# Attention with a hard score cut, then an eight-expert layer: where the value products of a pair of heads stand in the loop

## The chip, the cores and the metric

The kernel runs on one NeuronCore of a Trainium2 chip. The metric is the device time of one execution in microseconds (us). The engines of the core run side by side, each through its own list of instructions in order: TensorE (PE in the profile; PEld are its weight loads), VectorE (DVE), ScalarE (ACT), GpSimd (POOL) and SyncE (SP, which here only issues transfers).

## The reference

Two layers in a row. First attention over 8 batches x 8 heads, 576 positions, 64 wide, in which every score that lies more than `tau` under the largest of its row is dropped; then a layer of 8 experts, each of which takes at most 576 of the 4608 rows.

```python
# attention, per batch and head: q, k, v are [576, 64]
scores = scale * np.matmul(q, k.T)
thresh = np.max(scores, axis=-1, keepdims=True) - tau
scores = np.where(scores >= thresh, scores, -1e9)
attn = np.exp(scores - max); attn = attn / (sum + 1e-9)
x = attn @ v                      # the heads side by side: [4608, 512]
# experts
logits = x @ w_gate               # [4608, 8]; the best (row, expert) pairs first, 576 rows per expert
for e in range(8): out[mask_e] = np.maximum(x[mask_e] @ w1[e], 0) @ w2[e]
```

## The kernel before, in words

**Pairs, tiles and slots.** Two heads make a pair, so there are 32 pairs `p`, four to a batch `b`. The scores of a pair are worked in 9 tiles of 128 rows x 576 columns: eight full ones (128 queries of one head) and a short one, tile 8, with the last 64 queries of both heads. In all 288 tiles. The loop at the end of `attention` handles two tiles in one turn, a slot, numbered `s_`; two pairs are 18 tiles or 9 slots, so everything repeats every 9 slots, and below B is `9*(p//2)`: the even pair's short tile is scored in slot B+2, the odd one's in B+6, and the next two pairs begin at B+9.

**A tile's way.** TensorE writes the scores into PSUM (`sc`, line 69). VectorE multiplies them into SBUF with the row's extreme beside them (`z`, `nb`, line 74), ScalarE takes the exponential (line 86), VectorE zeroes what lies under the cut and sums the row (`pp` or `pm`, line 90), TensorE transposes the result in 64x64 blocks (`tb`, line 98), ScalarE copies that to `pt` (lines 113 and 115). One stage of a tile falls in one slot, the next in the slot after it or the one behind that. On TensorE a slot reads: scores of two tiles, in four slots of nine some left-over transposes (`left`, into spare columns of `sc`), value products, sometimes a small job, then the transposes of two older tiles.

**Value products.** The output of a pair, transposed, is made in two column halves `f`, of 256 and 320 queries, each with a PSUM bank of its own (`xo0`, `xo1`; `xo` in the profile). A half takes four *units* (`pv_unit`, line 146: two matmuls, one for each head, with 128 rows of keys and 64 output columns of the array) and its share of the *group* (`pl_unit`, line 154: four matmuls of 64x64 that add the last 64 keys, two for each half; their operand `pl` is copied out by ScalarE at lines 125, 127 and 128, the last of it in slots B+5 and B+9). When the group is through, ScalarE copies both banks to `xt` (line 155).

**What sets their order.** `push_pair` writes the units and the group of a pair into a queue when the pair's fourth tile has come back from the transposes, each with a condition (`when`) on the tiles that it needs. `columns` takes entries from the queue's head once a slot, behind the scores. The number that it takes is worked out from what is left of the pair and the slots up to `last_slot`, and it stops behind the group, which closes the pair. A unit that opens a half waits, in the program, until the bank's last reader stands in the list (`free_v`). Once a batch is through, small jobs (`aux`: the logits `lg_unit` twice, lines 173 and 175; two transposes `lgt_unit`, `lgm_unit`, lines 185 and 195; in the first two batches five `xt_unit`, line 207) run through `xo1` as well, one a slot, in slots where `xo1` is free (`whole`). What they leave in PSUM is read in the next slot, by ScalarE or VectorE (lines 178 to 217), ahead of that slot's line 74. The reads of the banks are put on their engines by `flush`, behind the scores of the next slot.

The last of the value products, the last logits and the sorting of rows to experts follow on each other; then comes the expert layer, which the change does not touch.

Of the kernel before, what the change touches and what calls it, by code (L numbers as in the profile page):

```python
# [13 lines left out]
AF = mybir.ActivationFunctionType  # L14
# [8 lines left out]
def attention(ctx, tc, qk, vl, tau, wgd, xrows, xts, Lg, nb_batches, ident, swap, R, after_first):  # L23
    nc=tc.nc
    V=nc.vector; A=nc.scalar; G=nc.gpsimd; T=nc.tensor
    NP=nb_batches*4; NT=NP*9
# [10 lines left out]
    LD={}  # L37
# [57 lines left out]
    PT={}; PL={}; TB={}  # L95
# [36 lines left out]
    have={}  # L132
# [3 lines left out]
    def bank_v(sh,n):  # L136
        banks[n].append([False])
        return ps_v.tile(sh,F32,name="xo%d"%n)
    def free_v(n): return banks[n][-1][0]
    def pv_unit(p,f,u):  # L140
        b,j=divmod(p,4)
        if b not in XT: XT[b]=wk.tile([128,4,S],F32,name="xt",bufs=XTB)
        if u==0: XO[p,f]=bank_v([128,512],f)
        xo=XO[p,f]; q=FQ[f]; v=LD[p]["v"]
        for h in range(2):
            T.matmul(xo[64*h:64*h+64,:q.stop-q.start],v[:,f,128*u+64*h:128*u+64*h+64],PT[p][:,h,u,q],start=(u==0),stop=False,skip_group_check=True)  # L146
    def pl_unit(p,fs=(0,1)):

        b,j=divmod(p,4); r=[]
        for f in fs:  # L150
            xo=XO.pop((p,f)); q=FQ[f]; n=q.stop-q.start
            for a in range(2):
                g=slice(64*a,64*a+64); h=a^f
                T.matmul(xo[64*h:64*h+64,:n],LD[p]["v"][g,f,512:576],PL[p][g,q],start=False,stop=True,skip_group_check=True)  # L154
            r.append((banks[f][-1],lambda xo=xo,q=q,n=n: A.activation(XT[b][:,j,q],xo[:,:n],AF.Copy)))
# [47 lines left out]
    def xt_unit(b,c,k=1):  # L203
        ps=bank_v([128,4,128],k)
        n=128 if c<4 else 64
        for j in range(4):
            T.transpose(ps[:n,j],XT[b][:,j,c*128:c*128+n],ident)  # L207
        early=b<nb_batches-NDEF-NBO
        if early: xr=wk.tile([128,XW],F32,name="xr",bufs=XRB)
        else: xr=wk.tile([128,2,S],F32,name="pp",bufs=PPB)[:,0,:XW]  # L210
        def ev():
            src=RD[b][:,:,2*c:2*c+2] if c<4 else RD["m",b][0:64]
            fv=xr[:n,512:XW].rearrange("p (j h) -> p j h",j=4); xv=xr[:n,:512].rearrange("p (j d) -> p j d",j=4)
            if early:
                V.tensor_copy(xv,ps[:n]); G.tensor_scalar(fv,src,1.0,0.0,op0=ALU.mult,op1=ALU.add)  # L215
# [10 lines left out]
    def push_pair(p):  # L226
        b,j=divmod(p,4)
        def when(n): return lambda: have.get((p,n),1<<30)+HOLD<=st["slot"]
        if p==NP-1:


            def left(f):
                for k,g in pl_unit(p,(f,)): g(); k[0]=True
            for f in range(2):
                for u in range(4): queue.append(("c",when("t3" if f==0 else "t8"),0 if u else f+1,lambda f=f,u=u: pv_unit(p,f,u),p))
                if f==0: queue.append(("n",when("t8"),False,lambda: rd_calc(b),p))
            for g in (lambda: left(0),lambda: left(1),lambda: lg_unit(b,0)(),lambda: lg_unit(b,1)(),lambda: lgt_unit(b)(),lambda: lgm_unit(b)()):
                queue.append(("n",when("pl"),False,g,p))
            queue.append(("n",lambda: not later,False,lambda: late.extend([lambda k,c=c: xt_unit(b,c,k) for c in range(5)]),p))
            return  # L240
        for f in range(2):
            for u in range(4): queue.append(("c",when("t3" if f==0 else "t8"),0 if u else f+1,lambda f=f,u=u: pv_unit(p,f,u),p))
# [12 lines left out]
    def flush():  # L255
        for k,g in later: g(); k[0]=True
        later.clear()
    def last_slot(p): return 9*(p//2)+(12 if p%2 else 8 if p<NP-2 else 7)
    def columns(all=False):
        c=[x[4] for x in queue if x[0]=="c"]  # L260
        if not c: n=9
        else: n=9 if all else max(1,c.count(c[0])//max(1,last_slot(c[0])-st["slot"]+1))
        while queue and queue[0][1]():
            k,_,first,g,p=queue[0]
            if k=="c":
                if n==0: return
                if first and not free_v(first-1): return
                n-=1
            queue.pop(0); r=g()
            if k=="c" and r:  # L270
                later.extend(r)
                return
    def whole():
        if aux and free_v(1) and st["slot"]>=st["last"]+aux[0][0]:
            r=aux.pop(0)[1](); st["last"]=st["slot"]
            later.append((banks[1][-1],r))

# [679 lines left out]
```

## Time and profile before

| | |
|---|---|
| time, median of 3 runs | 1000.09 us (997.43 to 1001.54) |
| the profiled execution | 1003.83 us, span 1001.9 us |
| attention's slots with TensorE full | 42.77 to 452.68 us |
| busy over the span | PE 964.3, DVE 781.2, ACT 633.0, POOL 261.9 us |
| mean granted TensorE clock | 0.983 |

Busy shares are over the whole program, of which attention's loop is a little under half; the stage itself is read by windows. A matmul of this kernel shows as two records, because each fp32 matmul makes two passes; so `x8` behind a group of rows is four matmuls. Matmuls overlap in the records: what one costs is read from the start of one row to the start of the next, not from its length. `64*128`, `64*64` and `128*64` ahead of a matmul's shape are the rows x columns of the array that it occupies.

### The profile page before, as it was taken

Reading aid. Unit: us, or ns where it says so; the run is one execution under the profiler, and the core shown is the slowest. Engines: PE = TensorE matmul, PEld = TensorE weight load, DVE = VectorE, ACT = ScalarE, POOL = GpSimd, SP = SyncE. Lnnn points to the kernel's source line nnn. Section 1 sums busy time; section 2 is a strip of 40 time slices with the busy share of each in tenths; the row PEclk is TensorE's granted clock in tenths of the full one; section 3 lists DMA queues with packets and bytes.
Section 4 is the critical chain, followed back from the end, with each engine's and each line's share of the span. In section 5 each row is a group of like instructions: output and inputs, shape, how many; then the busy total and the mean of one; then the engine's idle time right before and its main releaser. Section 6 shows DMA issues by size and latency. Waiting matters only on the chain.

```text
span 1001.9 us, 24115 instructions
## 1 busy us (share of the span) xinstructions
PE 964.3 (96%) x9141; PEld 710.4 (71%) x9141; DVE 781.2 (78%) x2158; ACT 633.0 (63%) x1257; POOL 261.9 (26%) x411
## 2 busy tenths in 40 slices
PE   7999999999999999998789999999999899999996
PEld 4555655655565555565679798897988879898895
DVE  7999999999999999995669778687787587525220
ACT  6899888888899898986545354253442344545340
POOL 2333443444233333330020213221303003220202
PEclk9999999999999999999979999999999899999998
DMA  6332251451533333203750605242434325241101
GB/s 250 97 119 84 83 182 58 177 184 61 176 111 120 99 117 106 97 3 141 260 199 20 224 30 183 84 152 93 153 106 135 120 70 172 100 156 56 40 11 42
DMA packets 35858, 116.98 MB, mean 117 GB/s; under 512 B 4384, under 2 KB 5024, under 8 KB 35232
## 3 DMA queue, kind: packets, MB, share of 16 engines
q1 hardware_dynamic: 28352, 92.85, 27.1%
q0 software_dynamic: 5888, 19.03, 6.0%
q10 hardware_dynamic: 1504, 3.59, 1.2%
q8 instruction: 72, 1.18, 0.5%
q14 instruction: 42, 0.34, 0.1%
HBM read 93.01 MB, written 21.38 MB: 114 GB/s over the span
## 4 chain that ended last, share of the span: by engine, by line
PE 84%; DVE 8%; issue 3%; DMA 2%; ACT 1%; another core or an unknown queue 0%; POOLq 0%; SPq 0%; DVEq 0%; ACTq 0%
PE pf L787 21%; PE pf L819 19%; PE sc L69 13%; PE xo L146 13%; PE tb L98 8%; DVE pp L90 2%; PE xo L154 2%; PE pt L732 2%; DVE z L74 2%; PE xo L207 1%; PE rps L440 1%; PE xo L173 1%; DMA out_dram<-y,idx 1%; PE sc L98 1%; DVE cmp L372 1%
## 5 line engine op out<-in xcount | busy, mean ns | idle before, releaser
L75 POOL TENSOR_SCALAR nb<-nb,taub 128x1 f32<-128x1 f32 x288 | 152.6, 530 | 286.2 <-DVE z L74 235.5
L86 ACT ACTIVATE pp<-z,nb 128x576 f32<-128x576 f32 x256 | 193.3, 774 | 39.6 <-DVE z L74 39.1
L74 DVE TENSOR_SCALAR_CACHE_REDUCE z<-sc 128x576 f32<-128x576 f32 x288 | 205.7, 750 | 14.6 <-PE sc L69 13.8
L90 DVE SCALAR_TENSOR_TENSOR pp<-z,nb,pp 128x576 f32<-128x576 f32 x256 | 199.8, 812 | 0.3
L819 PE MATMUL pf<-w2h,H 128*128 128x512 f32 x576 | 195.2, 402 | 0.7 <-DVE H L372 0.7
L69 PE MATMUL sc<-qk 64*128 64x288 f32 (+1 forms) x1280 | 181.2, 427 | 3.4 <-DVE z L74 1.5
L146 PE MATMUL xo<-pt,vt 128*64 128x320 f32 (+1 forms) x1024 | 155.7, 420 | 0.4 <-DVE xr L215 0.3
L113 ACT ACTIVATE pt<-tb 128x512 f32<-128x512 f32 x256 | 139.2, 589 | 3.3 <-PE tb L98 1.7
L819 PE MATMUL pf<-w2l,H 128*128 128x512 f32 x320 | 128.3, 401 | 0.0
L826 POOL DMA_INDIRECT out_dram<-y,idx x40 | 42.8, 1069 | 317.7 <-ACT y L822 244.2
L819 PEld LDWEIGHTS pf<-w2h,H 128*128 128x128 f32 x576 | 106.5, 189 | 21.5 <-DVE H L372 1.6
L69 PEld LDWEIGHTS sc<-qk 64*128 64x128 f32 (+1 forms) x1280 | 93.8, 179 | 33.7 <-DVE z L74 5.7
L98 PEld LDWEIGHTS tb<-ident,pp 64*128 64x128 f32 x2048 | 75.4, 139 | 58.0 <-ACT pp L86 20.1
L787 PE MATMUL pf<-xh,w1h 128*128 128x288 f32 (+2 forms) x512 | 112.0, 306 | 0.7 <-ACT xh L733 0.7
L787 PE MATMUL pf<-xl,w1h 128*128 128x288 f32 (+2 forms) x512 | 111.7, 304 | 0.0
L787 PE MATMUL pf<-xh,w1l 128*128 128x288 f32 (+2 forms) x512 | 111.7, 304 | 0.0
L822 ACT ACTIVATE y<-pf 128x512 f32<-128x512 f32 x40 | 23.9, 597 | 128.8 <-PE pf L819 125.3
L146 PEld LDWEIGHTS xo<-pt,vt 128*64 128x64 f32 x1024 | 60.7, 136 | 57.7 <-issue 27.4
L98 PE MATMUL tb<-ident,pp 64*128 64x64 f32 x2048 | 94.1, 229 | 5.0 <-ACT pt L113 4.8
L799 ACT ACTIVATE hf<-pf 128x576 f32<-128x576 f32 x56 | 36.5, 651 | 96.0 <-PE pf L787 83.0
L787 PEld LDWEIGHTS pf<-xh,w1h 128*128 128x128 f32 x512 | 83.9, 194 | 1.5 <-ACT xh L733 1.1
L787 PEld LDWEIGHTS pf<-xh,w1l 128*128 128x128 f32 x512 | 83.6, 193 | 0.2
(199 smaller groups left out, 1315.5 us busy)
## 6 DMA issues: line engine op xcount, KB each, us to landing
qk<-qk_dram SPq DMA_DIRECT2D x31, 864.0 KB, 4.7
vt<-vl_dram SPq DMA_DIRECT2D x32, 576.0 KB, 5.1
w2s<-w_dram SPq DMA_DIRECT2D x32, 512.0 KB, 5.5
w1s<-w_dram SPq DMA_DIRECT2D x28, 512.0 KB, 5.7
xrows<-pp SPq DMA_DIRECT2D x24, 260.0 KB, 2.8
xts<-xt SPq DMA_DIRECT2D x2, 1152.0 KB
pt<-xts SPq DMA_DIRECT2D x2, 1152.0 KB, 8.1
xrows<-xr SPq DMA_DIRECT2D x8, 260.0 KB, 2.0
```

Source lines behind the costliest of these rows:

```text
L69: T.matmul(sc[o,f,:HS], kd["q",h][r,c], kd["k",h][r,:],start=True,stop=True)
L74: V.tensor_scalar(z,SC.pop(t)[:,:,:HS],-0.125,None,op0=ALU.mult,op1=ALU.min,accum_out=nb[:,0:1])
L75: G.tensor_scalar(nb[:,1:2],nb[:,0:1],taub[:,0:1],None,op0=ALU.add)
L86: A.activation(pview(t),ZB[t].rearrange("p a b -> p (a b)"),AF.Exp,bias=NBI[t][:,0:1],scale=-1.0)
L90: V.scalar_tensor_tensor(pv,ZB.pop(t).rearrange("p a b -> p (a b)"),NBI[t][:,1:2],pv,op0=ALU.is_le,op1=ALU.mult,accum_out=den_of(p)[:,p%4, ...
L98: g=slice(64*r,64*r+64); T.transpose(o[:,r],x[r%len(x)][g],ident[g,g])
L113: A.activation(PT[p][:,i%2,:,(i//2)*128:(i//2+1)*128].rearrange("p k (r q) -> p r k q",r=2),tb,AF.Copy)
L146: T.matmul(xo[64*h:64*h+64,:q.stop-q.start],v[:,f,128*u+64*h:128*u+64*h+64],PT[p][:,h,u,q],start=(u==0),stop=False,skip_group_check=True)
L787: T.matmul(ps[:,h,:n],s[w][:,k,f*128:(f+1)*128],s[x][:,k,cols[h]],start=(i==0),stop=(i==11))
L799: A.activation(hf,ps[:,:,:HS],AF.Relu)
L819: T.matmul(ps[:,0,:],H[:,f,c:c+128],s[w][:,f],start=(f==0 and j==0),stop=e)
L826: G.indirect_dma_start(out=out,out_offset=IOA(ap=s["idx"][:n,t:t+1],axis=0),in_=y[:n],in_offset=None)
```

## The change

Each entry of the queue now carries the slot from which it may run, in place of its pair, and `columns` takes what is due. In each of the 9 slots there are two units, or one unit and the group: the even pair has its first half in slots B+4 and B+5, the group and one unit in B+6, two units in B+7 and one in B+8; the odd pair begins in B+8 with one unit, has two in B+9, one of each half in B+10, the group and one unit in B+11 and two units in B+12. The group stands in the slots that score a short tile (B+6 of its own two pairs, and B+11, which is slot B+2 of the next two), and it is the first thing behind the scores. It now closes the first half and opens the second one. The short tile is scored second in both cases; before, the even pair's was scored first. A half is copied out by itself, the first in the slot behind the group, the second in the slot behind its last unit. The last pair keeps its way: all units as soon as they can run, the group at the end. The number of matmuls, copies and transfers stays.

```diff
+    def evict(p,f):
+        b,j=divmod(p,4); xo=XO.pop((p,f)); q=FQ[f]
+        return banks[f][-1],lambda: A.activation(XT[b][:,j,q],xo[:,:q.stop-q.start],AF.Copy)
+    def open_v(p,f):
+        new=(p,f) not in XO
+        if new: XO[p,f]=bank_v([128,512],f)
+        return XO[p,f],new
-    def pv_unit(p,f,u):
+    def pv_unit(p,f,u,last):
...
-            T.matmul(xo[...],v[...],PT[p][:,h,u,q],start=(u==0),stop=False,skip_group_check=True)
-    def pl_unit(p,fs=(0,1)):
+            T.matmul(xo[...],v[...],PT[p][:,h,u,q],start=new,stop=last,skip_group_check=True)
+        if last:
+            if f==1: have[p,"pv"]=1
+            return [evict(p,f)]
+    def pl_unit(p,fs,last=()):
...
-                T.matmul(xo[...],LD[p]["v"][g,f,512:576],PL[p][g,q],start=False,stop=True,skip_group_check=True)
-            r.append((banks[f][-1],lambda xo=xo,q=q,n=n: A.activation(XT[b][:,j,q],xo[:,:n],AF.Copy)))
-        have[p,"pv"]=1
-        return r
+                T.matmul(xo[...],LD[p]["v"][g,f,512:576],PL[p][g,q],start=new,stop=f in last,skip_group_check=True)
+        return [evict(p,f) for f in last]
...
+        def v(f,u,at,last=False,first=False): queue.append(("c",when("t8" if f else "t3"),f+1 if first else 0,lambda: pv_unit(p,f,u,last),at))
+        B=9*(p//2)
...
-        for f in range(2):
-            for u in range(4): queue.append(("c",when("t3" if f==0 else "t8"),0 if u else f+1,lambda f=f,u=u: pv_unit(p,f,u),p))
-            if (f,j)==(0,3): queue.append(("n",when("t8"),False,lambda: rd_calc(b),p))
-        queue.append(("c",when("pl"),False,lambda: pl_unit(p),p))
+        for u in range(4): v(0,u,B+((8,9,9,10) if p%2 else (4,4,5,5))[u],False,u==0)
+        if j==3: queue.append(("n",when("t8"),0,lambda: rd_calc(b),p))
+        if p%2: v(1,0,B+10,False,True)
+        queue.append(("c",when("pl"),0 if p%2 else 2,lambda: pl_unit(p,(0,1),(0,)),B+(11 if p%2 else 6)))
+        for u in range(p%2,4): v(1,u,B+((0,11,12,12) if p%2 else (6,7,7,8))[u],u==3)
...
-    def last_slot(p): return 9*(p//2)+(12 if p%2 else 8 if p<NP-2 else 7)
     def columns(all=False):
-        c=[x[4] for x in queue if x[0]=="c"]
-        if not c: n=9
-        else: n=9 if all else max(1,c.count(c[0])//max(1,last_slot(c[0])-st["slot"]+1))
+        n=0
         while queue and queue[0][1]():
...
-                if n==0: return
-                if first and not free_v(first-1): return
-                n-=1
+                if not all and st["slot"]<at: return n
+                if first and not free_v(first-1): return n
+                n+=1
-            if k=="c" and r:
-                later.extend(r)
-                return
+            if k=="c" and r: later.extend(r)
...
         p8=[(t//9,n) for n,x in enumerate((tr_,ev_)) for t in x if t%9==8]
+        if sc_ and sc_[0]%9==8: sc_.reverse()
         for t in sc_: score(t)
```

In the lists below a unit's matmuls stand at line 146 before and 152 now, the group's at 154 and 162, the copies of the banks at 155 and 142, the small transposes' reads at 190, 191, 200, 201 and 196, 197, 206, 207. Here `x2` counts matmuls of two heads, so `x2` of `xo<-pt,vt` is one unit.

TensorE, slots B+6 to B+8 of pairs 2 and 3, from the scores of the odd pair's short tile, before:

```order
L69 MATMUL sc<-qk 64x288 x4
L146 MATMUL xo_831<-pt,vt 64x256 x2
L146 MATMUL xo_930<-pt,vt 64x320 x2
L98 MATMUL tb<-ident,pp 128x64 x16
L69 MATMUL sc<-qk 128x288 x4
L146 MATMUL xo_930<-pt,vt 64x320 x4
L98 MATMUL tb<-ident,pp 128x64 x16
L69 MATMUL sc<-qk 128x288 x4
L98 MATMUL sc<-ident,pp 128x64 x6
L146 MATMUL xo_930<-pt,vt 64x320 x2
L154 MATMUL xo_831<-pl,vt 64x256 x2
L154 MATMUL xo_930<-pl,vt 64x320 x2
```

and now:

```order
L69 MATMUL sc<-qk 64x288 x4
L162 MATMUL xo_831<-pl,vt 64x256 x2
L162 MATMUL xo_932<-pl,vt 64x320 x2
L152 MATMUL xo_932<-pt,vt 64x320 x2
L98 MATMUL tb<-ident,pp 128x64 x16
L69 MATMUL sc<-qk 128x288 x4
L152 MATMUL xo_932<-pt,vt 64x320 x4
L98 MATMUL tb<-ident,pp 128x64 x16
L69 MATMUL sc<-qk 128x288 x4
L98 MATMUL sc<-ident,pp 128x64 x6
L152 MATMUL xo_932<-pt,vt 64x320 x2
L152 MATMUL xo_1028<-pt,vt 64x256 x2
```

The group has moved up by two slots to the short tile's scores, and the next pair's first unit has moved into slot B+8.

TensorE, slots B+10 to B+12 of the same two pairs (B+11 scores the next even pair's short tile), before:

```order
L146 MATMUL xo_1074<-pt,vt 64x256 x4
L98 MATMUL tb<-ident,pp 128x64 x16
L69 MATMUL sc<-qk 64x288 x4
L69 MATMUL sc<-qk 128x288 x2
L146 MATMUL xo_1170<-pt,vt 64x320 x4
L98 MATMUL tb<-ident,pp 128x64 x16
L69 MATMUL sc<-qk 128x288 x4
L146 MATMUL xo_1170<-pt,vt 64x320 x4
L154 MATMUL xo_1074<-pl,vt 64x256 x2
L154 MATMUL xo_1170<-pl,vt 64x320 x2
```

and now:

```order
L152 MATMUL xo_1028<-pt,vt 64x256 x2
L152 MATMUL xo_1126<-pt,vt 64x320 x2
L98 MATMUL tb<-ident,pp 128x64 x16
L69 MATMUL sc<-qk 128x288 x2
L69 MATMUL sc<-qk 64x288 x4
L162 MATMUL xo_1028<-pl,vt 64x256 x2
L162 MATMUL xo_1126<-pl,vt 64x320 x2
L152 MATMUL xo_1126<-pt,vt 64x320 x2
L98 MATMUL tb<-ident,pp 128x64 x16
L69 MATMUL sc<-qk 128x288 x4
L152 MATMUL xo_1126<-pt,vt 64x320 x4
```

The short tile now stands behind the full one, and the group stands between it and the units in place of at the end of B+12.

The end of attention, VectorE, from the reads of the seventh batch's first small transpose (`lw`) to those of its second (`lwm`), before:

```order
L190 TENSOR_TENSOR lw<-xo_7058,rd 128x4x32 x2
L191 TENSOR_REDUCE Lg<-lw 128x32
L74 TENSOR_SCALAR z,nb<-sc 128x576 x2
L90 SCALAR_TENSOR_TENSOR pp,den<-z,nb,pp 128x576 x2
L200 TENSOR_TENSOR lwm<-xo_7111,rm 64x64
L201 TENSOR_REDUCE Lg<-lwm 64x8
```

and now:

```order
L197 TENSOR_REDUCE Lg<-lw 128x32
L74 TENSOR_SCALAR z,nb<-sc 128x576 x2
L90 SCALAR_TENSOR_TENSOR pp,den<-z,nb,pp 128x576 x2
L74 TENSOR_SCALAR z,nb<-sc 128x576 x2
L90 SCALAR_TENSOR_TENSOR pp,den<-z,nb,pp 128x576 x2
L74 TENSOR_SCALAR z,nb<-sc 128x576 x2
L90 SCALAR_TENSOR_TENSOR pm_100,den<-z,nb,pm_100 128x576
L90 SCALAR_TENSOR_TENSOR pp,den<-z,nb,pp 128x576
L74 TENSOR_SCALAR z,nb<-sc 128x576 x2
L90 SCALAR_TENSOR_TENSOR pp,den<-z,nb,pp 128x576 x2
L206 TENSOR_TENSOR lwm<-xo_7254,rm 64x64
L207 TENSOR_REDUCE Lg<-lwm 64x8
```

The second read comes four slots behind the first in place of one, since `xo1` is now in use in slots B+10 to B+12; it falls in a slot B+5. On ScalarE the copies of the second-last pair's two banks stood together ahead of the next two `pt` copies, before:

```order
L86 ACTIVATE pm_101<-z,nb 128x576
L113 ACTIVATE pt<-tb 128x2x4x64 x2
L155 ACTIVATE xt<-xo_7254 128x256
L155 ACTIVATE xt<-xo_7349 128x320
L113 ACTIVATE pt<-tb 128x2x4x64 x2
```

and now stand one slot apart:

```order
L86 ACTIVATE pm_101<-z,nb 128x576
L142 ACTIVATE xt<-xo_7249 128x256
L113 ACTIVATE pt<-tb 128x2x4x64 x2
L142 ACTIVATE xt<-xo_7351 128x320
L113 ACTIVATE pt<-tb 128x2x4x64 x2
```

More of the change, by code (lines that the diff above doesn't have):

```diff
@@ L139, in free_v @@
     def free_v(n): return banks[n][-1][0]
[L140 removed]
+    def evict(p,f):
[6 more added lines that the diff above has]
+    def pv_unit(p,f,u,last):
         b,j=divmod(p,4)
         if b not in XT: XT[b]=wk.tile([128,4,S],F32,name="xt",bufs=XTB)
[L143 to L144 removed]
+        xo,new=open_v(p,f); q=FQ[f]; v=LD[p]["v"]
         for h in range(2):
[L146 to L149 removed]
+            T.matmul(xo[64*h:64*h+64,:q.stop-q.start],v[:,f,128*u+64*h:128*u+64*h+64],PT[p][:,h,u,q],start=new,stop=last,skip_group_check=True)
+        if last:
+            if f==1: have[p,"pv"]=1
+            return [evict(p,f)]
+    def pl_unit(p,fs,last=()):
         for f in fs:
[L151 removed]
+            xo,new=open_v(p,f); q=FQ[f]
             for a in range(2):
                 g=slice(64*a,64*a+64); h=a^f
[L154 to L157 removed]
+                T.matmul(xo[64*h:64*h+64,:q.stop-q.start],LD[p]["v"][g,f,512:576],PL[p][g,q],start=new,stop=f in last,skip_group_check=True)
+        return [evict(p,f) for f in last]
     def bank_g(b,sh):
@@ L257, in flush @@
         later.clear()
-    def last_slot(p): return 9*(p//2)+(12 if p%2 else 8 if p<NP-2 else 7)
     def columns(all=False):
-        c=[x[4] for x in queue if x[0]=="c"]
-        if not c: n=9
-        else: n=9 if all else max(1,c.count(c[0])//max(1,last_slot(c[0])-st["slot"]+1))
+        n=0
         while queue and queue[0][1]():
-            k,_,first,g,p=queue[0]
+            k,_,first,g,at=queue[0]
             if k=="c":
-                if n==0: return
-                if first and not free_v(first-1): return
-                n-=1
+                if not all and st["slot"]<at: return n
+                if first and not free_v(first-1): return n
+                n+=1
             queue.pop(0); r=g()
-            if k=="c" and r:
-                later.extend(r)
-                return
+            if k=="c" and r: later.extend(r)
+        return n
     def whole():
-        if aux and free_v(1) and st["slot"]>=st["last"]+aux[0][0]:
+        if aux and free_v(1) and st["slot"]>=st["last"]+aux[0][0] :
             r=aux.pop(0)[1](); st["last"]=st["slot"]
```

12 lines of the change are left out of this document (6 added, 6 removed).

## The prediction

> **What bounds the kernel now.** I read the windows first, for the stage that the change touches, then TensorE's timeline over nine slots of that stage in which no small job runs (B = 99), then VectorE's and ScalarE's rows beside it. Columns of a window: its length, then busy time and instructions of PE, PEld, DVE, ACT and POOL, the granted clock, the share of the DMA engines, GB/s.
>
> ```profile
> 12.00:36.00 24.00, 20.94 (x259) 12.07 (x260) 24.00 (x69) 21.55 (x39) 8.66 (x18) 0.99 0.44 163
> 42.77:452.68 409.91, 409.06 (x4888) 240.16 (x4889) 398.24 (x1130) 366.30 (x709) 148.33 (x279) 1.00 0.33 111
> ```
>
> In the first slots VectorE is busy all the time and TensorE is not. From 42.77 to 452.68, which is 130 slots or 14.4 periods of nine, TensorE is idle for under 1 us, at full granted clock (1.00), and VectorE is busy 97% of the time. TensorE bounds, with VectorE close behind. A start in the timeline is us from the span's start; a row's cost is the distance to the next row's start.
>
> ```profile
> 335.39 1.19 PE L69 MATMUL sc<-qk 64*128 64x288 f32 x8
> ...
> 337.83 1.19 PE L69 MATMUL sc<-qk 64*128 64x288 f32 x8
> ...
> 340.63 1.35 PE L69 MATMUL sc<-qk 64*128 64x288 f32 x12
> 341.91 1.19 PE L146 MATMUL xo<-pt,vt 128*64 128x256 f32 x8
> ...
> 343.57 1.19 PE L69 MATMUL sc<-qk 64*128 64x288 f32 x8
> 344.69 1.30 PE L146 MATMUL xo<-pt,vt 128*64 128x320 f32 x8
> 345.92 0.71 PE L98 MATMUL tb<-ident,pp 64*128 64x64 f32 x16
> 346.47 1.19 PE L69 MATMUL sc<-qk 64*128 64x288 f32 x8
> 347.49 0.34 PE L98 MATMUL sc<-ident,pp 64*128 64x64 f32 x6
> 347.77 0.76 PE L146 MATMUL xo<-pt,vt 128*64 128x320 f32 x4
> 348.46 0.77 PE L154 MATMUL xo<-pl,vt 64*64 64x256 f32 x8
> 349.16 0.46 PE L98 MATMUL tb<-ident,pp 64*128 64x64 f32 x8
> ...
> 349.71 1.19 PE L69 MATMUL sc<-qk 64*128 64x288 f32 x8
> ...
> 352.51 1.34 PE L69 MATMUL sc<-qk 64*128 64x288 f32 x8
> 353.78 1.08 PE L146 MATMUL xo<-pt,vt 128*64 128x256 f32 x8
> 354.79 0.71 PE L98 MATMUL tb<-ident,pp 64*128 64x64 f32 x16
> 355.43 1.40 PE L69 MATMUL sc<-qk 64*64 64x288 f32 x12
> 356.76 1.30 PE L146 MATMUL xo<-pt,vt 128*64 128x320 f32 x8
> ...
> 358.54 1.19 PE L69 MATMUL sc<-qk 64*128 64x288 f32 x8
> ...
> 362.13 1.19 PE L69 MATMUL sc<-qk 64*128 64x288 f32 x8
> ```
>
> The period takes 26.74 us (335.39 to 362.13). Its slots are uneven: 2.44 the first (one unit), 3.59 the last (two units and the group). Costs that I use: two units of the second half 1.23 (344.69 to 345.92), one 0.69 (347.77 to 348.46), so a unit's streaming is 0.54 and 0.15 comes once, when the array leaves the units' 128*64 tiles. The group costs 0.70 (348.46 to 349.16): its longer matmuls stream 320 columns in two passes, as a unit does, and all four run beside each other, so 0.54 and again 0.16 for leaving the tiling. Scores ahead of units cost 1.12 (343.57 to 344.69), 1.02 ahead of transposes (346.47 to 347.49), which keep the tiling. Thus a change of tiling costs 0.1 to 0.16.
>
> **The change part by part.**
>
> *The group behind the short tile's scores.* Both use 64*64 tiles. Before, the array changed into 64*64 for the short scores and out again, and into it and out again for the group; now once. The group's 0.54 of streaming stays and its 0.16 goes: two groups a period, -0.32. The bounds: -0.70 x 2 if the group could hide altogether beside the scores; but these fill the array's four tiles themselves, so 0.54 is its floor and -0.32 the best; at the other end 0.70 as now, 0. I take -0.32, since the tiling is what the rows 1.02 and 1.12 tell apart.
>
> *The short tile second.* With the short tile first, the transposes ahead of it cost 0.64 (354.79 to 355.43) and the scores 1.33 (355.43 to 356.76), in all 1.97; with it second, 0.55 (345.92 to 346.47) and 1.28 (340.63 to 341.91), 1.83. One such slot a period: -0.14. VectorE's line 74 and ScalarE's exponentials follow the same order, VectorE's line 90 does not; the short tile's exponential has the two passes of line 74 in the next slot as cover, so I put nothing there.
>
> *Two units in every slot.* The units' sum is the same and every slot has one stretch of 128*64 before and after: 0 on TensorE by itself. The slots come to 2.79 to 3.06 (shortest, one unit of each half: 1.12 + 0.43 + 0.54 + 0.15 + 0.55, where 0.43 is half of 1.01 less 0.15, 353.78 to 354.79, and 0.55 the transposes at 345.92; longest, the group and a unit: 1.28 + 0.54 + 0.69 + 0.55), mean 26.13/9 = 2.90, where 26.13 is 26.74 less 0.46 and less a wait of 0.15, below. So the streaming saves 0.46 x 14.4 = 6.6 us. One more unit, 0.54, moves ahead of 42.77, into slots where VectorE covers it: -0.5.
>
> *VectorE as cover.* A turn of two line-74 and two line-90 passes:
>
> ```profile
> 350.46 0.76 DVE L74 TENSOR_SCALAR_CACHE_REDUCE z<-sc 128x576 f32<-128x576 f32 x1
> ...
> 351.82 0.82 DVE L90 SCALAR_TENSOR_TENSOR pp<-z,nb,pp 128x576 f32<-128x576 f32 x1
> ...
> 352.59 0.45 ACT L128 ACTIVATE pl<-sc 64x64 f32<-64x64 f32 x2
> ...
> 353.31 0.75 DVE L74 TENSOR_SCALAR_CACHE_REDUCE z<-sc 128x576 f32<-128x576 f32 x1
> ```
>
> 2.85 us (350.46 to 353.31), against slots of 2.79 to 3.06; the first pass starts 0.75 into the slot (349.71 to 350.46). In a period without small jobs VectorE falls behind by at most 0.1 and catches up. Before, in the slot of 2.44, it fell behind by 0.4.
>
> *Old waits.* The scores at 352.51 took 1.27 where 1.12 is the price: their second tile waited for ScalarE's last left-over copy (line 128, done at 353.04), 2.58 after VectorE's start of that slot. Both bank copies had gone ahead of it in that slot; now one does, and 0.3 less suffices. I take 0.15 a period, 14.4 times: -2.2.
>
> *New waits.* Small jobs put extra work ahead of VectorE's turn. Its prices, from start to start:
>
> ```profile
> 109.05 0.68 DVE L215 COPY xr<-xo 128x512 f32<-128x512 f32 x1
> 109.66 0.74 DVE L74 TENSOR_SCALAR_CACHE_REDUCE z<-sc 128x576 f32<-128x576 f32 x1
> ...
> 269.99 0.48 DVE L190 TENSOR_TENSOR lw<-xo,rd 128x128 f32<-128x128 f32 x2
> ...
> 271.05 0.74 DVE L74 TENSOR_SCALAR_CACHE_REDUCE z<-sc 128x576 f32<-128x576 f32 x1
> ...
> 273.99 0.23 DVE L200 TENSOR_TENSOR lwm<-xo,rm 64x64 f32<-64x64 f32 x1
> ...
> 274.55 0.76 DVE L74 TENSOR_SCALAR_CACHE_REDUCE z<-sc 128x576 f32<-128x576 f32 x1
> ```
>
> 1.06 for `lw`, 0.56 for `lwm`, 0.61 for `xr`. `lw` in slot B+10 leaves VectorE 1.05 late; slots of 3.06, 2.90 and about 3.1 wear that down to 0.45, and then `lwm` falls in a slot B+5 and makes it 1.0. The left-over copies of that slot end 2.2 to 2.3 after VectorE's start, so 3.0 into a slot of 2.8, and the second scores need them about 0.6 into the next one: they bear 0.4 to 0.5 of lateness. TensorE waits 0.5, in three batches or so: 1.5. An `xr` copy read in slot B+6 holds bank `xo1`, which the group opens 1.1 into that slot; where an earlier copy had VectorE 0.61 late, its turn ends 0.75 + 0.61 + 2.85 = 4.2 after the start of slot B+5, which with its own job I estimate at 3.4 (2.8 and one small job), so 0.8 into B+6, and the copy 0.61 later: a wait of 0.4, four times, 1.5. VectorE's lateness out of the first slots meets the shorter slots: 0.5. Sum +3.5; the other units queue behind the group on TensorE, so these waits count in full. Ends: 0 (all in lulls) and 13 (0.45 at each of 29 groups).
>
> *The end.* The last slots hang on ScalarE's `pt` copies.
>
> ```profile
> 455.19 0.71 PE L98 MATMUL tb<-ident,pp 64*128 64x64 f32 x16
> 455.94 1.08 ACT L113 ACTIVATE pt<-tb 128x512 f32<-128x512 f32 x2
> 457.08 0.71 PE L98 MATMUL tb<-ident,pp 64*128 64x64 f32 x16 [1.18 <-ACT pt L113]
> ...
> 458.95 0.77 PE L154 MATMUL xo<-pl,vt 64*64 64x256 f32 x8
> ...
> 459.64 0.71 ACT L155 ACTIVATE xt<-xo 128x256 f32<-128x256 f32 x2 [2.62 <-PE xo L154]
> ...
> 461.39 0.46 PE L98 MATMUL tb<-ident,pp 64*128 64x64 f32 x8 [1.34 <-ACT pt L113]
> ```
>
> Now a bank copy (0.3) stands ahead of the `pt` copies at 455.94, and VectorE arrives about 0.8 later by the late `lwm`; against that three units (1.76) replace two and the group (1.93), and one bank copy fewer stands at 459.64 (-0.3): +0.7. The expert layer moves as a whole.
>
> Sum: -6.6 - 0.5 - 2.2 + 3.5 + 0.7 = -5.1. The profiled execution, 1003.83 (span 1001.9 and 1.9 around it), would be 998.7; it lies 3.7 above the median of the runs, 1000.09, so I predict 995.0.
>
> *A rule that speaks against it.* The profile has, in the short tile's scores, the weight loads beside the matmuls:
>
> ```profile
> 355.43 0.21 PEld L69 LDWEIGHTS sc<-qk 64*64 64x64 f32 x8
> ```
>
> All eight loads, two for each tile, were through after 0.21, while the first passes still streamed; the second passes' weights loaded beside matmuls of the same rows. The Trainium skill (TensorE: Matmul & The Clock Gate, Part 3, The mechanism) says that weight loads overlap running matmuls only in other row groups. By that rule the group's first loads could not hide behind the short scores that hold all rows. That would be a rival; the trace does not bear the rule out.
>
> **The rivals.** *Exposed weights:* the group's first loads wait for the scores to end, at most the 0.21 of that row, twice a period: +6.0, time 1001.0, no change. Against it speak those loads themselves. *VectorE takes the gain:* at 398.24 of 409.91 it has 11.7 us of idle time in the stage, some of it only lulls; if half of the saving is turned into waits on it beyond the 3.5 I counted, -1.5, 998.6. For it: the shorter stage needs VectorE 98 to 99% busy. *Slower:* the group, now the first of the value products in its slot, waits for `pl` or for a bank in most slots, and the in-order engine with it: 0.45 x 29 = 13 in place of the 3.5 in the sum, time 1004.5. It decides once ScalarE's last left-over copy ends over 1.1 us into the next slot; at 353.04 it was 0.53 into it. *The waits vanish:* no new ones, -8.6 in all, 991.5.
>
> **How the numbers follow.** 0.5% of 1000 is 5 us, about what a measurement here can tell from no change. Forecast 0.62 (its own range 992 to 998, half of it faster by over 0.5%), no new waits 0.12, VectorE 0.13, exposed weights 0.05, slower 0.08. Faster: 0.12 + 0.31 + a little = 0.46; slower by over 0.5% 0.05 (part of that rival stays inside); the rest, 0.49, within. The range 990.5 to 1000.5 leaves out the slower rival, half of the exposed weights, and little below.
>
> **What would show it.** Right: in a period without small jobs, about 26.1 us from B+4's scores to the next B+4's; from the short scores to the units behind the group 1.8 where 1.28 stood before; line 162's rows 0.54 to their successor, the leaving included in the scores' old 1.28; no scores of 1.27 behind a slot B+9. Waits of 0.4 to 0.5 at line 162 where line 221 ran on VectorE in that slot, and at the scores behind `lwm`. Wrong: the group's row 0.7 or more ahead of the unit, or the scores in most slots waiting for line 74, which would mean that VectorE bounds; or slots that save their 0.46 and an end of attention that loses it again.

## The result and the profile after

The changed kernel takes 994.79 us (median of 8 runs, 989.31 to 997.56) where the kernel before, run beside it, takes 1000.63 (997.43 to 1002.43): a ratio of 0.994, with a 95% interval from 0.9915 to 0.9966. Two later sets of runs of the same kernel gave 0.9939 (0.9917 to 0.9962) and 0.9940 (0.9926 to 0.9955). The change makes the kernel 6 us faster; 995.0 had been forecast.

The profiled execution took 993.25 us, its span 991.4. First the windows of the changed kernel: slots 1 to 8, slots 9 and 10, and the 130 slots from 11 to 140, the same slots as 42.77 to 452.68 before. Slots are counted by `s_`; the columns are those of the windows in the prediction.

```profile
12.48:36.39 23.91, 20.69 (x261) 12.25 (x262) 23.91 (x67) 21.74 (x40) 8.63 (x18) 1.00 0.41 152
36.39:45.87 9.48, 7.66 (x75) 4.12 (x72) 9.08 (x38) 6.29 (x13) 3.71 (x8) 0.82 0.21 65
45.87:448.06 402.19, 401.72 (x4890) 242.82 (x4887) 395.41 (x1124) 366.43 (x705) 141.02 (x277) 1.00 0.33 113
```

The long stage went from 409.91 to 402.19, 7.7 us less, with TensorE idle for half a microsecond and VectorE busy 98% of it. Against that stand slots 9 and 10: 9.48 us, where the kernel before took 6.90 for them, and a granted clock of 0.82. I come back to them.

The next fence is TensorE's timeline of the changed kernel over nine slots without a small job, from one slot B+4 (51.82) to the next (77.93).

```profile
51.82 1.19 PE L69 MATMUL sc<-qk 64*128 64x288 f32 x8
...
57.48 1.35 PE L69 MATMUL sc<-qk 64*128 64x288 f32 x12
58.65 0.71 PE L162 MATMUL xo<-pl,vt 64*64 64x256 f32 x8
59.29 0.76 PE L152 MATMUL xo<-pt,vt 128*64 128x320 f32 x4
59.98 0.71 PE L98 MATMUL tb<-ident,pp 64*128 64x64 f32 x16
60.53 1.19 PE L69 MATMUL sc<-qk 64*128 64x288 f32 x8
...
69.20 1.19 PE L69 MATMUL sc<-qk 64*128 64x288 f32 x8
70.32 1.19 PE L152 MATMUL xo<-pt,vt 128*64 128x256 f32 x8
...
77.93 1.19 PE L69 MATMUL sc<-qk 64*128 64x288 f32 x8
```

The period is 26.11 us (before 26.74, forecast 26.13). A group slot (57.48 to 60.53) takes 3.05: scores 1.17, the group 0.64, the unit 0.69, transposes 0.55. From the short scores to the unit behind the group it is 1.81, where the scores alone had cost 1.28 and the group 0.70 elsewhere. That sum is as forecast; its parts are not, for the prediction had the group at 0.54 and all of the leaving with the scores. The scores of slot B+10, behind the last left-over copies, take 1.12 (69.20 to 70.32) and no longer 1.27. The stage has 14 such scores: before, five of them waited (1.27 to 1.43), now one does (1.29, in slot 127), and the others take 1.12 in both kernels.

Where small jobs run, the group does wait. Slot 60 is the worst of them; TensorE, then VectorE in the slots 59 and 60:

```profile
196.68 1.45 PE L69 MATMUL sc<-qk 64*128 64x288 f32 x12
197.95 0.61 PE L162 MATMUL xo<-pl,vt 64*64 64x256 f32 x4
198.85 0.76 PE L162 MATMUL xo<-pl,vt 64*64 64x320 f32 x4 [0.28 <-DVE xr L221]
199.53 0.76 PE L152 MATMUL xo<-pt,vt 128*64 128x320 f32 x4
```

```profile
194.59 0.23 DVE L206 TENSOR_TENSOR lwm<-xo,rm 64x64 f32<-64x64 f32 x1
...
198.11 0.68 DVE L221 COPY xr<-xo 128x512 f32<-128x512 f32 x1
```

The read of `lwm` makes VectorE late, its `xr` copy starts 1.43 into slot 60 (198.11 less 196.68), and the group's second half cannot open the bank `xo1` until it is done. From 197.95 to 199.53 is 1.58 where 0.64 is the price. In the whole stage I count seven such waits: at the group 0.21, 0.07, 0.94 and 0.46 (slots 33, 42, 60 and 96; in slot 96 the bank is held for a read of `lwm` and not for an `xr` copy), at the scores 0.10, 0.23 and 0.17 (slots 60, 123, 127), 2.2 us in all. Counted in the same way, as what a row takes above its usual cost, the kernel before has 2.5: 1.9 at the scores and the rest at units.

Slots 9 and 10 of the changed kernel, on TensorE; the last number ahead of the arrow is idle time before the row:

```profile
38.82 0.54 PE L98 MATMUL tb<-ident,pp 64*128 64x64 f32 x12
40.49 0.76 PE L69 MATMUL sc<-qk 64*128 64x288 f32 x4 [1.13 <-DVE z L74]
41.94 1.33 PE L69 MATMUL sc<-qk 64*128 64x288 f32 x4 [0.69 <-ACT pl L128]
43.20 2.19 PE L152 MATMUL xo<-pt,vt 128*64 128x256 f32 x8
45.32 0.71 PE L98 MATMUL tb<-ident,pp 64*128 64x64 f32 x16
```

Two waits, one for VectorE and one for ScalarE's left-over copy, and then work at half speed: the units' row is 2.12 to its successor where 1.12 is usual. On VectorE the router's set-up (line 376) fills 37.25 to 39.68 ahead of the slot's first pass:

```profile
37.25 0.17 DVE L376 MEMSET onesb<- 128x128 bf16 x1
...
39.68 0.75 DVE L74 TENSOR_SCALAR_CACHE_REDUCE z<-sc 128x576 f32<-128x576 f32 x1
```

That block, `R.consts`, stands in the queue behind the first pair's value products, and these end in slot 8 in both kernels. Before, `columns` stopped behind the group that closed the pair; the block was taken in slot 9 and ran on VectorE in slot 10, and TensorE waited 1.15 for it once. The changed `columns` has no such stop, so the block is taken in slot 8, right behind the pair's last unit, and runs in slot 9. The pair's last value products, the block's first row and the wait, before:

```profile
34.62 0.77 PE L154 MATMUL xo<-pl,vt 64*64 64x256 f32 x8
...
39.52 0.17 DVE L372 MEMSET onesb<- 128x128 bf16 x1
...
42.77 1.43 PE L69 MATMUL sc<-qk 64*64 64x288 f32 x12 [1.15 <-DVE z L74]
```

In the changed kernel the last unit starts in a row of slot 8 (33.42 to 36.39) that it shares with the next pair's first unit:

```profile
34.72 1.19 PE L152 MATMUL xo<-pt,vt 128*64 128x320 f32 x8
```

The end: in the changed kernel the `pt` copies are waited for as before, 1.59 and 1.19 (1.18 and 1.34 before), and from the last scores to the last logits it is 14.58 (448.06 to 462.64) where it was 14.50.

```profile
452.86 0.71 PE L98 MATMUL tb<-ident,pp 64*128 64x64 f32 x16 [1.59 <-ACT pt L113]
...
456.85 0.46 PE L98 MATMUL tb<-ident,pp 64*128 64x64 f32 x8 [1.19 <-ACT pt L113]
...
462.64 1.05 PE L179 MATMUL sc<-xt,wg 128*32 128x256 f32 x8
```

So in this pair of profiles attention, from slot 1 to the last logits, went from 455.38 to 450.15. Behind it the two differ by 6.0 as well (534.7 and 528.8), with the same code. That part took 524.2 to 530.5 in the eleven other profiles of this study, 525.1 in the one of them that has the old order of units; I put nothing of it down to the change.

### The profile page after: what moved, and what is told of

Read it like the earlier page. It is cut to its first block, busy times and chain, and to the rows that moved or that the text cites. A ratio compares the mean times of both kernels' runs of the same rounds, so it can differ in the third digit from the quotient of the medians.

```text
span 991.4 us, 24055 instructions
## 1 busy us (share of the span) xinstructions
PE 955.4 (96%) x9141; PEld 709.3 (72%) x9141; DVE 782.1 (79%) x2158; ACT 635.1 (64%) x1257; POOL 261.0 (26%) x411
## 3 DMA queue, kind: packets, MB, share of 16 engines
q10 hardware_dynamic: 1504, 3.59, 1.2%
q8 instruction: 72, 1.18, 0.5%
## 4 chain that ended last, share of the span: by engine, by line
PE 83%; DVE 8%; issue 3%; DMA 3%; ACT 2%; POOLq 0%; SPq 0%; DVEq 0%; ACTq 0%
PE pf L791 21%; PE pf L823 19%; PE sc L69 13%; PE xo L152 12%; PE tb L98 8%; DVE pp L90 2%; DVE z L74 2%; PE pt L736 2%; PE xo L162 2%; PE xo L213 1%; PE rps L444 1%; PE xo L179 1%; DMA out_dram<-y,idx 1%; PE sc L98 1%; DVE cmp L376 1%
## 5 line engine op out<-in xcount | busy, mean ns | idle before, releaser
L75 POOL TENSOR_SCALAR nb<-nb,taub 128x1 f32<-128x1 f32 x288 | 149.7, 520 | 286.6 <-DVE z L74 246.4
```

The lines of the kernel that those rows point to most:

```text
L75: G.tensor_scalar(nb[:,1:2],nb[:,0:1],taub[:,0:1],None,op0=ALU.add)
```

## The experiments

I read each run by the starts of the slots in its profile, which repeat far better than times do: the stage of 130 slots took 402.19 us in three profiles of the changed kernel, the same to the hundredth. By their times alone the kernels with the unit ahead, the short tile first, the uneven units and the three jobs later can't be told from the changed one, since their intervals overlap with its own; what is said of them rests on the slots of one profile each. All numbers in us.

| kernel | slots 1-8 | slots 9-10 | 130 slots | end | attention | ratio to before (95%) |
|---|---|---|---|---|---|---|
| before | 24.07 | 6.90 | 409.91 | 14.50 | 455.38 | 1 |
| changed, first profile | 23.91 | 9.48 | 402.19 | 14.58 | 450.15 | 0.9940 (0.9915 to 0.9966) |
| changed, second | 23.90 | 7.91 | 402.19 | 14.58 | 448.57 | 0.9939 (0.9917 to 0.9962) |
| changed, third | 23.90 | 7.91 | 402.19 | 14.57 | 448.57 | 0.9940 (0.9926 to 0.9955) |
| before, short tile second | 24.08 | 6.90 | 408.91 | 14.50 | 454.40 | 0.9992 (0.9982 to 1.0002) |
| changed, unit ahead of the group | 24.07 | 7.74 | 405.75 | 14.42 | 451.99 | 0.9963 (0.9949 to 0.9977) |
| changed, short tile first | 23.91 | 8.00 | 405.70 | 14.31 | 451.93 | 0.9976 (0.9956 to 0.9996) |
| changed, uneven units | 23.91 | 9.79 | 405.06 | 14.51 | 453.27 | 0.9970 (0.9954 to 0.9985) |
| changed, three jobs later | 23.90 | 7.91 | 401.64 | 14.72 | 448.16 | 0.9946 (0.9925 to 0.9967) |
| changed, set-up one slot later | 23.90 | 6.94 | 402.78 | 14.58 | 448.19 | one run |
| changed, set-up at the end | 23.90 | 5.60 | 402.17 | 14.58 | 446.24 | 0.9931 (0.9915 to 0.9948) |
| the same, second profile | 23.91 | 5.59 | 402.15 | 14.58 | 446.23 | 0.9901 (0.9886 to 0.9916) |
| the same, and 48 matmuls in a gap behind attention | 23.91 | 5.59 | 402.19 | 14.58 | 446.27 | 0.9924 (0.9893 to 0.9955) |

**One part alone: the short tile second.**

```diff
 # in the kernel before
+        if sc_ and sc_[0]%9==8: sc_.reverse()
         for t in sc_: score(t)
```

> The kernel before with one part of the change alone: the short tile's scores second in the slot of the even pair; units and groups stay where they were. Theory (a change of tiling costs 0.10 to 0.16, and this order leaves one out): a quiet period of nine slots 26.60 where it was 26.74, the stage of 130 slots 0.14 x 14.4 = 2.0 shorter than 409.91, about 407.9; time 998 to 999. Rival (the short tile's later exponential and left-over copies make VectorE late): the period shortens, but waits at the next slot's scores give it back, stage 409.5 to 411, time unchanged. If the change's gain is mostly this order and not the place of the group, the stage falls by 5 or more.

The quiet period fell from 26.74 to 26.61, so the price of the order, 0.14, holds. But the stage fell by 1.0 only, half of what 14.4 periods would give: the waits at the scores, 0.51 in slot 56 and 0.13 to 0.31 in twelve others, come to 3.0 where the kernel before has 1.9. The rival was half right. Order alone is worth one microsecond, and the time does not show it.

**The same work, with the unit ahead of the group.**

```diff
-        if p%2: v(1,0,B+10,False,True)
-        queue.append(("c",when("pl"),0 if p%2 else 2,lambda: pl_unit(p,(0,1),(0,)),B+(11 if p%2 else 6)))
-        for u in range(p%2,4): v(1,u,B+((0,11,12,12) if p%2 else (6,7,7,8))[u],u==3)
+        for u in range(4):
+            v(1,u,B+((10,11,12,12) if p%2 else (6,7,7,8))[u],u==3,u==0)
+            if u==p%2: queue.append(("c",when("pl"),0,lambda: pl_unit(p,(0,1),(0,)),B+(11 if p%2 else 6)))
```

> The changed kernel, with the order inside the two group slots turned round: scores, then the one 128*64 unit, then the group of 64*64 tiles, so that the same work stands in the same slots, but the group is no longer behind 64*64 scores. Theory (the gain of the group's place is the change of tiling that it saves): one more change per group, 0.15 to 0.16, twice a period: a quiet period 26.41 where it was 26.11, the stage 4.3 to 4.6 longer than 402.19, about 406.7; time 998 to 1000. Rival 1 (the gain comes from the even spread of the units over the slots): stage within 1 of 402.2. Rival 2 (the group waits less when a unit stands ahead of it, for pl and for its bank): the waits of 0.94, 0.45 and 0.21 at the group go, but the unit opens the same bank, so at most 0.6 is won back, stage 406.

TensorE's timeline of this kernel, one group slot:

```profile
408.55 1.35 PE L69 MATMUL sc<-qk 64*128 64x288 f32 x12
409.83 0.76 PE L152 MATMUL xo<-pt,vt 128*64 128x320 f32 x4
410.52 0.77 PE L162 MATMUL xo<-pl,vt 64*64 64x256 f32 x8
411.22 0.71 PE L98 MATMUL tb<-ident,pp 64*128 64x64 f32 x16
411.76 0.46 PE L69 MATMUL sc<-qk 64*128 64x288 f32 x2
```

The slot takes 3.21 (408.55 to 411.76) in place of 3.05: the scores pay 1.28 again and the group 0.70, and 0.16 is one change of tiling. The stage is 3.6 longer, not 4.6: about 1.0 comes back, because some of the waits at the group vanish when a unit stands ahead of it, more than the 0.6 that the second rival allowed. Of the two ends that the prediction left for the group, this settles the price: 0.16 each, and the place of the group carries 3.6 net of the stage's 7.7.

**The short tile first again.**

```diff
-        if sc_ and sc_[0]%9==8: sc_.reverse()
```

> The changed kernel with the short tile first again in the slot of the even pair, so that full scores stand between the short scores and the group of that slot; the odd pair's slot is as changed. Theory (each change of tiling costs 0.10 to 0.16): 0.14 for the order itself and 0.16 for the group, 0.30 a period: quiet period 26.41 where it was 26.11, stage 4.3 longer, 406.5. Rival (only the order of the two score tiles matters): 0.14 a period, 404.2. Rival 2 (neither): 402.2.

A group slot of the even pair, TensorE in that kernel:

```profile
69.76 0.71 PE L98 MATMUL tb<-ident,pp 64*128 64x64 f32 x16
70.41 1.40 PE L69 MATMUL sc<-qk 64*64 64x288 f32 x12
71.74 0.77 PE L162 MATMUL xo<-pl,vt 64*64 64x256 f32 x8
72.44 0.76 PE L152 MATMUL xo<-pt,vt 128*64 128x320 f32 x4
```

The transposes ahead cost 0.65 in place of 0.55, the scores 1.33 in place of 1.17, the group 0.70 in place of 0.64: 0.32 for the two changes of tiling that come back, once a period. The stage grew by 3.5 where 14.4 times that is 4.6; again near 1.0 of waits went away. The order of the two tiles, worth 1.0 alone, is worth over three times that once the group relies on it.

**The even spread undone.**

```diff
-        for u in range(p%2,4): v(1,u,B+((0,11,12,12) if p%2 else (6,7,7,8))[u],u==3)
+        for u in range(p%2,4): v(1,u,B+((0,11,11,12) if p%2 else (6,6,7,8))[u],u==3)
```

> The changed kernel with the even spread undone around the groups: a group's slot holds the group and two units, the one or two slots behind it one unit less, as before the change; the group stays behind the short scores. Theory (the even spread is worth nothing in TensorE's streaming, and about 0.15 a period in waits): the stage of 130 slots 2.2 longer than 402.19, 404.4, the loss at the scores behind the long and short slots. Rival 1 (even spread is the main gain, since VectorE's turn of 2.85 doesn't fit a slot of 2.3): a slot of 2.3 ends in a wait of 0.3 to 0.5, twice a period, stage 411 to 416. Rival 2 (VectorE catches up in the long slot, nothing is lost): 402 within 0.5.

One long slot, one short, and the scores that wait (TensorE):

```profile
69.61 1.50 PE L69 MATMUL sc<-qk 64*128 64x288 f32 x8
71.04 1.19 PE L152 MATMUL xo<-pt,vt 128*64 128x256 f32 x8
...
72.71 1.35 PE L69 MATMUL sc<-qk 64*128 64x288 f32 x12
...
76.30 1.19 PE L69 MATMUL sc<-qk 64*128 64x288 f32 x8
...
78.65 0.70 PE L69 MATMUL sc<-qk 64*128 64x288 f32 x4
```

Slots of 3.59 and 2.35 stand in place of 3.05 and 2.90, the streaming is the same, and the scores at 69.61 cost 1.43. The stage is 2.9 longer, all of it in waits: summed over the slots they come to 5.0 where the changed kernel has 2.2. The theory (2.2) was near in size, but had put the loss at the scores alone: at the group the waits went from 1.7 to 3.0, at the scores from 0.5 to 1.7. The short slot itself holds no wait of 0.3 to 0.5, so rival 1 falls, and VectorE does not make up for all of it, so rival 2 does too.

**Three small jobs moved.**

```diff
-        if aux and free_v(1) and st["slot"]>=st["last"]+aux[0][0] :
+        if aux and free_v(1) and st["slot"]>=st["last"]+aux[0][0] and st["slot"] not in (32,59,95):
```

> The changed kernel with no small job in slots 32, 59 and 95 (slots B+5 whose xr copy or job holds bank xo1 at the group of the next slot, right behind an lwm read); those jobs run at later slots. Theory (the group waits for the bank that the xr copy on VectorE still holds, when VectorE is late by an earlier small job): the rows of the group at 112.7, 196.7 and 309.4, long by 0.21, 0.94 and 0.45, come back to 0.64, the stage of 130 slots is 1.6 shorter, 400.6, if the moved jobs find slots without such a pair. Rival (the group waits for ScalarE's left-over copies in pl): the three rows stay long. Rival 2 (the moved jobs only shift the wait): other groups long by 0.4 to 0.9, stage 402. By time alone 1.6 can't be told from nothing.

The groups of slots 33, 60 and 96 came back to 0.64, so it was the bank, as the theory said. But other slots now wait, as the second rival said: 0.83 at the group of slot 132, 0.25 in slot 105, 0.23 at the scores of slot 60. The stage gained 0.55. The row at 418.42 is the second half of the group in slot 132:

```profile
417.64 0.61 PE L162 MATMUL xo<-pl,vt 64*64 64x256 f32 x4
418.42 0.76 PE L162 MATMUL xo<-pl,vt 64*64 64x320 f32 x4 [0.17 <-DVE rm L187]
419.11 0.76 PE L152 MATMUL xo<-pt,vt 128*64 128x320 f32 x4
```

**The router's set-up in the last slots.** The casts and memsets go into a function that is called where the last pair's `rd_calc` stands; `w8`, which is needed earlier, and GpSimd's part stay.

```diff
-            queue.append(("n",when("t8"),0,lambda: rd_calc(b),p))
+            queue.append(("n",when("t8"),0,lambda: (rd_calc(b),R.consts_tail()),p))
```

> The changed kernel with the router's set-up on VectorE (26 instructions, 2.45 us, at 37.25 to 39.7) taken out of the first slots: only the 0.1 to 0.7 cast of w8 stays there, the rest is done in the last slots, where VectorE is idle for 6.9 us. Theory (slots 9 and 10, 4.11 and 5.38, are long because that block stands ahead of VectorE's turn of slot 9, which makes the left-over copies late, and because TensorE then runs at half clock): slots 9 and 10 about 2.9 each, slot 1 to slot 11 in 29.5 to 30 us where it took 33.39, granted clock 1.00 throughout; attention 3 to 4 shorter, time 991 to 992. Rival (VectorE is late there by the first slots' own backlog, not by the block): slots 9 and 10 still 3.5 to 5, gain under 1.5. Rival 2: the block in the last slots delays the end, attention's end 1 to 2 later there.

Slots 9 and 10, the windows of this kernel and of the changed one in its third profile, which ran on the same chip as the second profile here:

```profile
36.31:41.91 5.60, 5.60 (x75) 3.55 (x72) 5.60 (x18) 5.58 (x13) 3.21 (x8) 1.00 0.36 110
```

```profile
35.37:43.27 7.90, 6.07 (x74) 3.60 (x72) 7.85 (x35) 5.68 (x13) 3.18 (x8) 1.00 0.26 78
```

TensorE is busy throughout, and nothing is lost at the end (14.58). 3.9 us of attention are won against the first profile of the changed kernel, 2.3 against the two others; the slots came out a little under the 2.9 each that I expected. The time gained less than I had expected: 987.03 beside 994.06 for the kernel before is 7.0, where 991 to 992 beside 1000.63 would have been 9.

**The set-up one slot later, where it stood before the change.**

```diff
-        for u in range(4): v(0,u,B+((8,9,9,10) if p%2 else (4,4,5,5))[u],False,u==0)
+        for u in range(4):
+            v(0,u,B+((8,9,9,10) if p%2 else (4,4,5,5))[u],False,u==0)
+            if (p,u)==(1,2): queue.append(("n",lambda: True,False,R.consts,p))
...
-        if (b,j)==(0,0): queue.append(("n",lambda: True,False,R.consts,p))
```

> The changed kernel with the router's set-up one slot later in VectorE's order, behind slot 9's passes, where it stood before the change. Theory (the block costs more one slot earlier, because there it also makes the left-over copies late, which hold the second score tile): slots 9 and 10 in 6.9, as before the change, where the changed kernel takes 7.91 or, with a window at half clock, 9.48; full clock, since one gap of 1.15 leaves no window of 3.41 less than half busy. Rival (the block costs its 2.4 wherever it stands in the first slots): 7.9.

6.94, as before the change. So the block costs 1.3 there and 2.3 one slot earlier; the further 1.0 is the left-over copies, which in slot 9 stand behind the late exponential on ScalarE; slot 10 has none. Part of that returns: the stage is 0.6 longer (402.78), since VectorE comes out of slot 10 later.

**The changed kernel again**, twice, and beside it the better one.

> The changed kernel once more, beside the variants below. Slots 9 and 10 took 9.48 in its first profile, 3.41 of them at half clock, and 7.91 in the kernel with three jobs moved, which is the same up to slot 32 and kept the full clock. Theory (the stall of 1.13 and 0.69 costs 2.3, and the half clock another 1.57 when both gaps fall into one window of 3.41): 7.9 or 9.5, nothing between; from slot 1 to the end of attention 448.6 or 450.2, 6.8 or 5.2 less than before, ratio 0.993 to 0.995. Rival (the ramp differs by its own loads): slots 9 and 10 anywhere from 7 to 10.

> The changed kernel beside the one above. Theory: slots 9 and 10 in 7.91 or 9.48, the stage of 130 slots 402.19 as in both earlier profiles; from slot 1 to the end of attention 6.8 or 5.2 less than before, ratio 0.993 to 0.995.

> The kernel with the router's set-up in the last slots of attention again, on one chip with the changed kernel. Theory: from slot 1 to the end of attention 446.2, 2.3 less than the changed kernel at full clock there and 3.9 less where a window of 3.41 runs at half clock; time 2.3 to 3.9 below the changed kernel's, ratio to the kernel before about 0.991. Rival (what is won ahead is lost behind attention, where gathers and routing begin sooner): less than 1 below the changed kernel.

7.91 both times; attention 448.57 both times. On one chip the kernel with the set-up at the end took 984.99 and the changed one 989.00, both against 995.41 for the kernel before; their intervals, 0.9886 to 0.9916 and 0.9926 to 0.9955, do not meet. It is the better kernel. The profiles show 2.3 of the 4.0; behind attention the two took 524.5 and 524.2, so nothing was lost there, and where the other 1.7 lies stays open: windows at half clock in slots 9 and 10, in some executions, would make up to 1.57 of it.

**TensorE kept busy in the routing's gap.**

```diff
 # in the kernel with the set-up at the end
+            if r==0 and t==0:
+                for _ in range(48): T.matmul(ps[:,0,:],R.ones,R.ones,start=True,stop=True)
```

> The kernel with the router's set-up moved to the last slots of attention, and beside that 48 matmuls of ones (128x128) in TensorE's gap of 3.3 us ahead of the first expert's transposes, whose result is overwritten. Theory (the rest of the span behind attention, 525 to 535 us for the same work, differs by stretches at half clock, 10 to 24 us of them, that start in the routing's gaps): the stretch of 10 to 14 us at half clock around that gap is cut to 3.4 or 6.8, the rest falls from 526 to 522 to 524, time 983 to 985. Rival (the rest differs by the experts' gathers, not by the clock): no change, or the 48 matmuls delay the transposes, rest 526 to 528.

The windows of this kernel, behind the gap:

```profile
503.62:507.03 3.41, 3.41 (x17) 3.15 (x15) 3.41 (x12) 2.00 (x7) 0.00 (x0) 0.50 0.81 279
507.03:520.00 12.97, 12.74 (x114) 12.02 (x114) 10.64 (x36) 6.25 (x16) 0.00 (x0) 1.00 0.26 90
```

The stretch at half clock around that gap is down to one of 3.41, but the part behind attention took 529.8, among the longest; in the second profile without the 48 matmuls the stretch was 6.83 and that part took 524.5. Ratio 0.9924 (0.9893 to 0.9955), no better than without. So that part's length does not follow from that stretch. Why it differs by 6 between executions of the same code stays open.

## Why the prediction was right

Right in the time (995.0, measured 994.79), partly by errors that cancel. Step by step:

- *The group behind the short scores, the short tile second* (-6.6): right. The period without jobs came out at 26.11, forecast 26.13. Without the old wait of 0.15 it fell by 0.48, forecast 0.46, which is 6.9 in the stage; one change of tiling is 0.16, twice over. The Trainium skill (TensorEngine Tiling (Array Packing), Key Properties) says that a change of the tiling mode drains TensorE; the trace agrees so far that each change costs time, 0.16 us here, though no row shows the drain itself.
- *One unit ahead of the stage* (-0.5): right. Slots 1 to 8 did not grow (24.07 to 23.91), and the unit is missing from the stage.
- *Old waits* (-2.2): right in size, but by luck. I had read one wait of 0.15 in one period and put it into every period. It stood in 5 of 14, 0.9 in all; the rest of the 2.5 that the kernel before waits lay elsewhere. Behind B+9 one wait is left. Putting the unevenness back brings 2.9 of waits, about half of them at the group.
- *New waits* (+3.5, of which 3.0 in the stage): right in mechanism, too large. The group waits for `xo1` in four slots, as said, for 1.7 in all (forecast 1.5), though for 0.07 to 0.94 each and not 0.4. The scores behind `lwm` wait 0.5 together, after two of its reads, and not 0.5 in each of three batches. In the stage the four terms made -6.3; it was -7.7. Of the difference the waits make 1.1 (2.5 before and 2.2 now is -0.3, where old and new together had been put at +0.8) and the streaming 0.3.
- *VectorE's lateness out of the first slots* (+0.5): the step that failed. I had looked at VectorE as cover for the unit moved there, and not at what the stop behind the group had held back: without it the set-up behind the first pair's value products is taken one slot earlier. That cost 1.0 against before (7.91 for 6.90) and, in the first profile, 1.57 more at half clock.
- *The end* (+0.7): +0.1. The `pt` copy waits 0.4 longer at the first place, and the second wait and three units in place of two and the group give it back.

Together -5.1 was forecast for attention. It was -5.2 in the first profile and -6.8 in the two others, and -6 in the times. That the first profile comes so near is luck: the stage gave 1.4 more than forecast and the end 0.6, and slots 9 and 10 took 2.6 where 0.5 had been put.

Of the rivals, exposed weights did not come true: scores and group together take 1.81, which is the scores at 1.28 and the group's 0.54 of streaming, so no load stands exposed. VectorE, at 98% of the stage, did not take the gain. The group waits in four slots of 29, not in most.

## What to carry to other kernels

A change of the array's tiling has a price of its own (0.16 us here), so work of one tiling belongs side by side; but what it saves arrives only where no wait takes its place: the short tile's order alone gave 1.0 of the 2.0 that its tiling is worth, because waits at the scores grew by 1.1. When the rule by which a queue is emptied changes, look at everything that the old rule held back: here a set-up block came one slot earlier and landed ahead of copies that others wait for. And a job with no deadline belongs where its engine is idle, not where it happens to fit in the code.

## What the hardware showed that I had not expected

The half clock after the stall in slots 9 and 10 came in one profile of the changed kernel and not in the two others, with the same waits of 1.13 and 0.69. The clock's records change only in steps of 3.41 us, on a grid that lies differently in each execution. Windows on that grid, TensorE's busy time and the granted clock: first profile, second profile, and the kernel with uneven units, which has the same block ahead of waits at the same two places (1.44 and 0.69).

```profile
38.54:41.95 3.41, 1.59 (x24) 1.00 0.01 5
41.95:45.36 3.41, 3.41 (x14) 0.50 0.01 2
```

```profile
37.21:40.62 3.41, 1.99 (x26) 1.00 0.13 45
40.62:44.03 3.41, 3.00 (x35) 1.00 0.01 2
```

```profile
38.92:42.33 3.41, 1.28 (x22) 1.00 0.00 0
42.33:45.75 3.42, 3.42 (x14) 0.50 0.01 2
```

Where both gaps fell into one window, TensorE was busy for 1.59 or 1.28 of 3.41 (47% and 38%) and the next window ran at half clock; where the grid cut through them, 1.99 (58%) kept it full. The 13 profiles of this study say the same: between 12 and 960 us, all 28 windows at full clock that TensorE filled to 53% or less were followed by one at half clock, and of the more than 3500 that it filled further only one was, at 62%. The Trainium skill (TensorE: Matmul & The Clock Gate, Part 1) has the grid, free-running windows of 3413 ns, but asks for an idle window before the clock is halved; here no window was idle, and a busy share of 47% was already too little. The wait itself costs 2.3 us, and the half clock, when it comes, another 1.57.
